# Norms and v issued later, blocks 12 to 15 choosing slots as four, and own buffers for the rows of blocks 16 to 21

## The chip, the cores and the metric

The kernel runs on one core of a Trainium2 chip. The core has five engines, each with its own queue of instructions that it works through in order: PE (TensorE, matrix products into PSUM), DVE (VectorE, elementwise work and reductions), ACT (ScalarE, copies out of PSUM and activations), POOL (GpSimd, masks, memory clearing, and the DMAs that scatter rows by an index) and SP (SyncE, which only issues the other DMAs). They wait for each other, and for DMAs, through semaphores. The metric is the device time of one execution in microseconds, lower being better.

## What is computed

A recurrence over 768 positions for 4 batches and 8 heads, whose result goes through a layer of 8 experts with one expert for each row:

```python
for t in range(S):                                   # _attn_ref: q, k, v of (4, 8, 768, 48)
    kt, vt, bt = (k_n[:, :, t], v[:, :, t], beta[:, :, t, None])     # k_n = k / (|k| + 1e-6)
    y[:, :, t] = np.einsum('bhd,bhde->bhe', q[:, :, t], state)
    v_old = np.einsum('bhde,bhd->bhe', state, kt)
    state = state + bt[:, :, :, None] * np.einsum('bhd,bhe->bhde', kt, vt - v_old)
...
x = attn_out.transpose(0, 2, 1, 3).reshape(B * S, H * D)             # 3072 rows of 384
logits = x @ w_gate                                                  # _moe_ref
expert_idx = np.argmax(logits, axis=1)
gate_w = probs[np.arange(N), expert_idx]                             # softmax of the logits
for e in range(E):
    h = np.maximum(x[expert_idx == e] @ w1[e], 0.0)                  # 384 x 1024
    out[expert_idx == e] = gate_w[mask, None] * (h @ w2[e])          # 1024 x 384
```

## The kernel before

The 768 positions are cut into 6 chunks (`tb`) of 128, and with 4 batches (`b`) this gives 24 blocks, `n = 4 * tb + b`, each for all 8 heads. The instructions of each engine are written out in the order in which the loop at line 1006 (`for t in range(NN + LAG)`) emits them; no scheduler moves them. A block lives for several steps `t`: in steps n to n+3 its four quarters of 32 positions go through `residual` and `apply`, quarter q in step n+q, so that each step holds quarters of four blocks. `residual(t)` makes PE compute what the state and earlier quarters predict (lines 451, 463), and DVE subtracts it from v (line 470). `apply(t)` multiplies by the inverse of a triangular matrix (line 478), and ACT copies the result out as u (line 483). `finish(n)` begins in step n+3: the output y (lines 498, 518), the update of the state (products 508, ACT copies st, line 512), the copy yt (522). Its last part runs in step n+4: PE turns y into a row of x together with the logits (line 548), ACT copies the row into a buffer (line 549), DVE reduces the logits (535).

Beside this run, a few pieces at each of the seven places of a step (`beside(t, i)`):

- `lanes(tb)`, the inverses of the next chunk, on DVE alone (lines 374 to 418), at counts fixed for each place; `prepare(tb)` before it, which also makes the norms of k. Line 351 turns the norms, line 354 writes them with four DMAs of 32 partitions into `nt_all`. In `scale_v` DVE scales v by them (line 428, every second step). v lies in a ring of 8 slots; `load_v(tb, q)` loads a quarter of a chunk into slots that `apply` of an earlier step was the last to read.
- `emit_slots`, the choice of slots. For a group of `w` blocks (4 up to block 11, pairs for 12 to 15, one from block 16 on) DVE finds each row's expert (lines 589 to 606), PE counts with a few products (line 559), DVE turns the counts into row numbers (625 `pos`, 650 `sli`), and POOL scatters each row to `xg` in DRAM by its number (line 658). The groups stand in a list `fine`, and after its first five steps only the group at the head of the list goes on. Groups of more than one block let out two scatters in a step.
- From step 20 on `pieces`: raw expert weights come in, ACT casts them to a high part (`w1h`, `w2h`, line 697) and DVE makes the low part (line 698). From step 23 on the first expert starts (`early`), for which line 737 reads `xg` back once all scatters up to block 17 have landed.

The buffers of the rows: two of two rows each for the first pair of a group (tag `row`), two for the second pair of a group of four (`rowb`). Blocks 16 to 21 use the two `row` buffers, one row at a time, in turns. A buffer is written again when the scatter that reads it has landed.

Steps are numbered by line 470: step 10 begins at 120.10 us of the trace, step 14 at 157.44, step 17 at 180.24, step 18 at 190.93, step 19 at 199.97, step 20 at 206.77, step 21 at 214.48, step 22 at 222.94, step 23 at 230.39, step 24 at 242.11. Behind step 26 come the eight experts, almost all on PE, up to 506 us.

Of the kernel before, what the change touches and what calls it, by code (L numbers as in the profile page):

```python
# [8 lines left out]
F32 = mybir.dt.float32  # L9
# [9 lines left out]
B, H, S, D = 4, 8, 768, 48  # L19
C = 128  # L20
NT = S // C
NB = C // 32
# [9 lines left out]
NN = NT * B  # L32
# [4 lines left out]
ROW = DM + E + 2  # L37
# [5 lines left out]
def deltanet_moe(ctx, tc, qT, kT, kr, v, beta, w_gate, w1, w2, out):  # L43
    nc = tc.nc
# [67 lines left out]
    W0 = 42  # L112
    WD = {1: 12, 2: 15, 3: 14, 4: 3}
    W1 = 8
    W4 = 12
    DM2 = 0
    DEF = 2
    AH = 3
# [12 lines left out]
    rp = ctx.enter_context(tc.tile_pool(name="rp", bufs=1, side="left"))  # L131
    lp_ = ctx.enter_context(ExitStack())
    ep_ = ctx.enter_context(ExitStack())
    lp = lp_.enter_context(tc.tile_pool(name="lp", bufs=1, side="left"))
    fp = ep_.enter_context(tc.tile_pool(name="fp", bufs=1, side="right"))
# [21 lines left out]
    nt_t = lp.tile([128, (NT * B + LAG) * H], F32, name="nt_all")  # L157
# [153 lines left out]
    def full(x):  # L311
        return x[:, 0:1024].rearrange("p (r c) -> p r c", c=32)
# [5 lines left out]
    def prepare(tb):  # L318

        T = tiles[tb]  # L320
        if tb == 0:
            T["lg"] = fp.tile([128, LW], F32, name="lg0", tag="lg", bufs=2)
            tiles["mark"] = nc.vector.transpose(out=full(T["lg"]), in_=tiles["dg"]).ins
            yield
        lg = T["lg"]
        lw = T["lw"]
        ss, s0, r0 = (lp.tile([128, 32], F32, name=f"{n_}{tb}", tag=n_) for n_ in ("ss", "s0", "r0"))
        nc.vector.tensor_scalar(out=ss, in0=lg[:, 0:1024:33], scalar1=1e-36, scalar2=None, op0=ALU.max)
        for _ in range(6 if tb > 1 else 1):
            yield  # L330
        nc.scalar.activation(out=s0, in_=ss, func=AF.Sqrt)
        yield
        nc.vector.reciprocal(r0, s0)
        yield
        nc.vector.tensor_tensor(out=r0, in0=r0, in1=ss, op=ALU.mult)
        yield
        nc.vector.tensor_tensor(out=s0, in0=s0, in1=r0, op=ALU.add)
        yield
        nc.vector.tensor_scalar(out=s0, in0=s0, scalar1=0.5, scalar2=1e-6, op0=ALU.mult, op1=ALU.add)
        yield  # L340
        nc.vector.reciprocal(r0, s0)
        yield
        nc.vector.tensor_tensor(out=ss, in0=r0, in1=bl[:, tb, :], op=ALU.mult)
        yield
        nc.vector.tensor_tensor(out=lw.rearrange("p a b -> p (a b)")[:, 0:1024:33], in0=ss, in1=r0, op=ALU.mult)
        yield
        nc.vector.tensor_tensor(out=r0, in0=ss, in1=r0, op=ALU.mult)
        yield
        def norms():
            sn = lp.tile([128, 32], F32, name=f"sn{tb}", tag="sn")  # L350
            nc.vector.transpose(out=sn, in_=s0)
            for q in range(NB):
                p = slice(32 * q, 32 * q + 32)
                nc.sync.dma_start(out=nt_t[p, (B * tb + q) * H:(B * tb + q) * H + 32], in_=sn[p])
            yield

        nc.vector.tensor_tensor(out=blocks(lg), in0=blocks(lg), in1=r0.rearrange("p (f r) -> p f r", f=2).unsqueeze(3)
                                .broadcast_to([128, 2, HB, HB]), op=ALU.mult)
        T["scaled"] = True
        yield  # L360
        yield from norms()
        T["nt"] = True

# [77 lines left out]
    def uview(n):  # L441
        return us[n].rearrange("t (h d) -> t h d", h=H)
# [44 lines left out]
    def finish(n):  # L487

        tb, b = n // B, n % B
        last = tb == NT - 1  # L490
        st, u = st_t[b], uview(n)
        qt, pm = qt_t[n % QTL], pm_t[n % QSL]
        yp = [pss.tile([128, 512], F32, name=f"yp{tb}_{b}_{j}", tag=f"y{j}")[:, 0:2 * C].rearrange("p (n c) -> p n c", n=2)
              for j in range(2)]
        for p in range(NP):
            for a in range(2):
                x = slice(64 * (a ^ p % 2), 64 * (a ^ p % 2) + 64)
                nc.tensor.matmul(yp[p % 2][x, p // 2], lhsT=st[64 * a:64 * a + D, p, 64 * a:64 * a + 64],  # L498
                                 rhs=qt[64 * a:64 * a + D, p, :], start=(p < 2), stop=True,
                                 tile_position=(64 * a, x.start), skip_group_check=True)  # L500
        if n + QTL < NN:
            load_qt(n + QTL)
        yield
        if not last:
            sb = sb_[b // 2][:, b % 2]
            for h in range(H):
                r = slice(64 * (h % 2), 64 * (h % 2) + D)
                nc.tensor.matmul(sb[r, h // 2, :], lhsT=tiles[tb][b]["kn"][:, h], rhs=u[:, h, :],
                                 start=(tb == 0 and b == 2 and h < 2), stop=True, skip_group_check=True)
            for a in range(2):  # L510
                r = slice(64 * a, 64 * a + D)
                nc.scalar.copy(out=st[r, :, r], in_=sb[r])  # L512
            if n + NB_ < NN - B:
                load_ku(n + NB_)
        yield
        for h in range(H):
            p, r = h // 2, 64 * (h % 2 ^ h // 2 % 2)
            nc.tensor.matmul(yp[p % 2][r:r + D, p // 2], lhsT=u[:, h, :], rhs=pm[:, h, :],  # L518
                             start=False, stop=True, skip_group_check=True)
        yt = lp.tile([128, NP, C], F32, name=f"yt{tb}_{b}", tag="yt", bufs=2)  # L520
        for j in range(2):
            nc.scalar.copy(out=yt[:, j::2], in_=yp[j])  # L522
        yield
        w = 1 if n >= NN - W1 else 2 if n >= W4 else 4
        j, m = n % w, min(w, 2)
        if j == 0:
            tiles["rows"] = []
            tiles["rl"] = lp.tile([128, w, E], F32, name=f"rl{tb}_{b}", tag=f"rl{w}", bufs=2)
        if j % m == 0:
            pool, tag = (fp, "rowb") if j >= 2 else (rp, "row") if n < NN - 2 else (xq_[0], "row")  # L530
            t = pool.tile([128, 2 if n < NN - 2 else 1, ROW], F32, name=f"row{tb}_{b}", tag=tag, bufs=2)
            tiles["rows"].append(t[:, 0:m])
        xp = emit_x(n, yt, tiles["rows"][-1][:, j % m])
        yield
        nc.vector.tensor_reduce(out=tiles["rl"][:, j], in_=xp[:, :, 2 * D:].rearrange("t p e -> t e p"), axis=AX.X, op=ALU.add)
        if j == w - 1:
            fine.append(emit_slots(tb, b - w + 1, w, tiles["rows"], tiles["rl"]))
# [192 lines left out]
    put, put_t, off = [], [], []  # L730
    wq, xq_, XR, last, psk_, fine, X0 = [], [], {}, [], [], [], {}
# [274 lines left out]
    for t in range(NN + LAG):  # L1006
        if t < NN and t % B == 0 and t > 0:
            while queue and queue[0][0] <= t // B:
                inverses(1, t)
            if t == NN - B:  # L1010
                ep_.close()
                wq.append(ep.enter_context(tc.tile_pool(name="wr", bufs=1, side="right")))
                xq_.append(ep.enter_context(tc.tile_pool(name="xq", bufs=1, side="right")))
                W = pieces()
                run(W)
        mask()
        residual(t)
        if LAG <= t < NN - KTL + LAG:
            load_kt(t - LAG + KTL)
        run(fin)  # L1020
        beside(t, 0)
        n = len(fine)
        run(fin)
        if len(fine) > n:
            tiles["at"] = 0
            run(fine[-1], 5)
        if B <= t + 1 < NN:
            scale_v(t + 1)
        if t < B - 1:
            clear_slots()  # L1030
        if t + 1 < NN + LAG and not B <= t + 1 < NN:
            scale_v(t + 1)
        if t + 1 < NN:
            clear_u(t + 1)
        beside(t, 1)
        dummy(WD.get(t, 0))
        copies = apply(t)
        run(copies, 2)
        for tb in range(1, NT):
            for i in range(NB):  # L1040
                if t == max(B * (tb - 1) + i - 1, 0):
                    load_v(tb, i)
        beside(t, 2)
        fin = finish(t - LAG) if t >= LAG else iter(())
        run(fin)
        chunk(qs_, t)
        beside(t, 3)
        run(fin)
        beside(t, 4)
        run(fin)  # L1050
        beside(t, 5)
        for _ in range(2 if t < 2 else 1):
            chunk(ks_, t)
        beside(t, 6)
        clear_slots()
    i = 0
# [141 lines left out]
    if True:  # L1198
# [20 lines left out]
        row = nc.values_load(gii[0:1, 0:1], min_val=0, max_val=E * N)  # L1219
# [51 lines left out]
        for f in range(KF):  # L1271
# [4 lines left out]
                                     in_=yo, in_offset=None, bounds_check=N - 1, oob_is_err=False)  # L1276
# [48 lines left out]
```

## Time and profile before

| | us |
|---|---|
| median of 3 runs (lowest to highest) | 518.15 (517.04 to 521.36) |
| the profiled execution | 522.53 |
| its span in the trace | 520.7 |
| PE busy in it | 484.5 (93%) |
| DVE busy | 337.7 (65%) |
| ACT busy | 254.7 (49%) |
| POOL busy | 112.8 (22%) |

All times of rows are microseconds from the start of the span. A row of the timeline gives the start, the time taken, the engine (PE is the matmul itself; its weight loads are a line of their own and not shown here), the line of the kernel, the operation, the tile written and those read, the shape, how many instructions are merged in the row, and in brackets how long the engine had been idle before it and what ended that. The start of a merged row is that of its first instruction. SPq is the queue of SP: for a DMA issue its time includes waiting that lies between merged issues. PEclk is the TensorE clock that was granted, as a share of the full 2.4 GHz; 0.50 is 1.2 GHz.

### The profile page before, as it was taken

The numbers are of one execution on the slowest core, as the hardware profiler recorded it, in microseconds if no ns is written. First come the engines' busy times: TensorE is split into PE (matmuls) and PEld (weight loads), VectorE is DVE, ScalarE is ACT, GpSimd is POOL, SyncE is SP. The second block draws the span as 40 slices with busy tenths as digits, with TensorE's granted clock in tenths as the row PEclk, the third lists the DMA queues.
The fourth block names the chain that finished last, engine by engine and source line by source line (L and its number), as shares of the span: only waits on it lengthen the run. The fifth ranks groups of instructions, "written<-read, shape, count | busy, mean of one in ns | idle before, by whom it ended". The sixth has DMA issues, their size and how long they took to land.

```text
span 520.7 us, 17340 instructions
## 1 busy us (share of the span) xinstructions
PE 484.5 (93%) x7286; PEld 434.8 (83%) x7291; DVE 337.7 (65%) x975; ACT 254.7 (49%) x539; POOL 112.8 (22%) x148
## 2 busy tenths in 40 slices
PE   7699899998998979999999999999999999999991
PEld 5656678887887868777889999999999999999991
DVE  2989959898689998465322976465756646565310
ACT  3413556674675645775343564444436444444210
POOL 6010121242242333323122001203030210303121
PEclk9999999997999989997999999999999999999997
DMA  6589747757554443762041595473847547481000
GB/s 197 121 194 256 188 140 192 220 157 183 145 156 107 136 121 107 244 198 91 18 102 68 163 239 157 121 183 115 203 124 164 160 134 161 141 197 36 13 18 27
DMA packets 74844, 74.14 MB, mean 142 GB/s; under 512 B 46649, under 2 KB 62506, under 8 KB 74764
## 3 DMA queue, kind: packets, MB, share of 16 engines
q1 hardware_dynamic: 71308, 63.45, 46.5%
q0 software_dynamic: 3456, 9.57, 5.1%
q8 instruction: 58, 0.95, 0.8%
q14 instruction: 22, 0.18, 0.1%
HBM read 54.25 MB, written 19.42 MB: 141 GB/s over the span
## 4 chain that ended last, share of the span: by engine, by line
PE 50%; issue 1%; ACT 1%; DMA 1%; SPq 1%; DVE 1%; POOL 1%; ACTq 0%; POOLq 0%
PE h L813 21%; PE y L824 18%; PE y L1131 4%; PE xp L548 1%; PE yp L518 1%; DMA w1r<-in_w_dram 1%; SPq L737 1%; PE ks L451 1%; PE ks L478 1%; PE pq L284 1%; PE ks L463 1%; PE xt L889 0%; POOL out_dram L827 0%; PE yp L498 0%; ACT pm L296 0%
## 5 line engine op out<-in xcount | busy, mean ns | idle before, releaser
L824 PE MATMUL y<-w2h,hx 128*128 128x384 f32 x352 | 93.2, 339 | 0.4 <-DVE hx L817 0.4
L827 POOL DMA_INDIRECT out_dram<-yo,idx x32 | 40.3, 1259 | 197.5 <-ACT yo L1126 113.0
L824 PEld LDWEIGHTS y<-w2h,hx 128*128 128x128 f32 x352 | 64.0, 188 | 1.2 <-DVE hx L817 1.1
L483 ACT COPY u<-ks 32x384 f32<-32x384 f32 x96 | 45.1, 469 | 33.7 <-PE ks L478 23.6
L813 PE MATMUL h<-xh,w1l 128*128 128x448 f32 x168 | 61.3, 365 | 0.0
L813 PE MATMUL h<-xh,w1h 128*128 128x448 f32 x168 | 61.2, 365 | 0.0
L813 PE MATMUL h<-xl,w1h 128*128 128x448 f32 x168 | 61.1, 363 | 0.0
L824 PE MATMUL y<-w2l,hx 128*128 128x384 f32 x176 | 59.4, 337 | 0.0
L698 DVE TENSOR_TENSOR w2l<-w2r,w2h 128x768 fp32r<-128x768 f32 x32 | 30.6, 957 | 40.6 <-ACT w2h L697 40.0
L817 DVE SCALAR_TENSOR_TENSOR hx<-h,hx 128x448 fp32r<-128x448 f32 (+1 forms) x64 | 37.5, 587 | 29.8 <-ACT hx L816 29.2
L816 ACT ACTIVATE hx<-h 128x448 fp32r<-128x448 f32 (+1 forms) x64 | 33.2, 518 | 44.8 <-PE h L813 44.8
L303 POOL TENSOR_SCALAR_AFFINE_SELECT pm<-pm 128x1024 f32<-128x1024 f32 x24 | 26.3, 1095 | 91.0 <-DVE tb L374 24.9
L1126 ACT ACTIVATE yo<-y,gt 128x384 f32<-128x384 f32 x22 | 12.8, 582 | 64.5 <-PE y L824 36.6
L451 PE MATMUL ks<-st,kt 112*32 112x96 f32 x768 | 43.5, 253 | 0.7 <-ACT st L512 0.5
L451 PEld LDWEIGHTS ks<-st,kt 112*32 112x32 f32 x768 | 32.4, 111 | 5.5 <-issue 1.9
L385 DVE TENSOR_TENSOR lw<-lw,ta 128x31 f32<-128x31 f32 (+7 forms) x96 | 36.6, 381 | 0.2
L284 PE MATMUL pg<-kt 48*128 48x128 f32 x384 | 31.7, 317 | 5.2 <-DMA kt<-in_kT_dram 4.2
L698 DVE TENSOR_TENSOR w1l<-w1r,w1h 128x1024 fp32r<-128x1024 f32 x24 | 29.4, 1225 | 9.0 <-ACT w1h L697 8.6
L478 PE MATMUL ks<-v_all,wt 32*32 32x48 f32 x1536 | 25.8, 206 | 10.1 <-DVE v_all L470 6.6
L284 PEld LDWEIGHTS pg<-kt 48*128 48x128 f32 x384 | 28.3, 222 | 8.3 <-issue 5.2
L658 POOL DMA_INDIRECT xg<-row,sli x22 | 22.6, 1028 | 58.0 <-ACT yt L522 20.4
L478 PEld LDWEIGHTS ks<-v_all,wt 32*32 32x32 f32 x1536 | 21.4, 107 | 16.4 <-DVE v_all L470 9.8
(166 smaller groups left out, 1038.3 us busy)
## 6 DMA issues: line engine op xcount, KB each, us to landing
w1r<-in_w_dram SPq DMA_DIRECT2D x24, 512.0 KB
w2r<-in_w_dram SPq DMA_DIRECT2D x32, 384.0 KB
xg<-zrow SPq DMA_DIRECT2D x14, 394.0 KB
kt<-in_kT_dram SPq DMA_DIRECT2D x24, 224.0 KB
qt<-in_qT_dram SPq DMA_DIRECT2D x24, 224.0 KB
xr<-xg SPq DMA_DIRECT2D x28, 168.0 KB
ku<-in_kr_dram SPq DMA_DIRECT2D x20, 192.0 KB
v_all<-in_v_dram SPq DMA_DIRECT2D x15, 192.0 KB
```

Of the source, the lines that this page charges most:

```text
L284: ins = nc.tensor.matmul(pg[a][:, p], lhsT=kt[r, p], rhs=xt[r, p], start=True, stop=True, tile_position=(64 * a, 0), skip_group_check=True)
L303: ins = nc.gpsimd.affine_select(out=pm, in_=pm, compare_op=ALU.is_gt, fill=0.0, base=0, pattern=[[0, H], [1, C]], channel_multiplier=-1)
L385: tiles["mark"] = noted(nc.vector.tensor_tensor(out=y, in0=y, in1=x, op=ALU.subtract))
L451: nc.tensor.matmul(ks[32 * q:32 * q + 32, 2 * p:2 * p + 2, :], lhsT=kt_t[n % KTL][0:RP, p, 32 * q:32 * q + 32], rhs=st_view(n % B, p), sta ...
L478: ins = nc.tensor.matmul(ks[r, h, :], lhsT=tiles[n // B]["wt"][r, n % B * H + h, :], rhs=vn[r, h, :], start=True, stop=True, tile_position ...
L483: nc.scalar.copy(out=uview(n)[r], in_=ks[r])
L698: nc.vector.tensor_tensor(out=lo, in0=src, in1=hi.bitcast(F32), op=ALU.subtract)
L813: nc.tensor.matmul(ps, lhsT=w[:, d, fs], rhs=x_[:, d], start=(n == 0), stop=(n == len(terms) - 1))
L816: nc.scalar.activation(out=hh, in_=ps, func=AF.Relu)
L817: nc.vector.scalar_tensor_tensor(out=hl, in0=ps, scalar=0.0, in1=hh.bitcast(F32), op0=ALU.max, op1=ALU.subtract)
L824: nc.tensor.matmul(ps, lhsT=h(f)[h_], rhs=w2[w][:, f, :], start=(n == 0), stop=(n == len(terms) - 1))
L827: nc.gpsimd.indirect_dma_start(out=out, out_offset=bass.IndirectOffsetOnAxis(ap=idx, axis=0), in_=yo, in_offset=None, bounds_check=N - 1, ...
```

## The change

Three edits:

1. The four DMAs of the norms, for chunks 2 to 5, are no longer issued where `prepare` ends, but put into the list `off`, due in step 4(tb-1)+1 at place 2; and a v quarter of chunks 2 to 5 is loaded one step later.
2. `W4` goes from 12 to 16, so blocks 12 to 15 choose slots as one group of four. No pairs are left.
3. Buffers: blocks 14 and 15 share one new buffer of two rows (`rowb`, in pool `lp`), and blocks 16 to 21 alternate between two new buffers of one row (`rowc`).

```diff
-    W4 = 12
+    W4 = 16
...
-            for q in range(NB):
-                p = slice(32 * q, 32 * q + 32)
-                nc.sync.dma_start(out=nt_t[p, (B * tb + q) * H:(B * tb + q) * H + 32], in_=sn[p])
+
+            def spread():
+                for q in range(NB):
+                    p = slice(32 * q, 32 * q + 32)
+                    nc.sync.dma_start(out=nt_t[p, (B * tb + q) * H:(B * tb + q) * H + 32], in_=sn[p])
+
+            if tb < 2:
+                spread()
+            else:
+                off.append(((B * (tb - 1) + 1, 2), spread))
+                off.sort(key=lambda x: x[0])
             yield
...
-            pool, tag = (fp, "rowb") if j >= 2 else (rp, "row") if n < NN - 2 else (xq_[0], "row")
-            t = pool.tile([128, 2 if n < NN - 2 else 1, ROW], F32, name=f"row{tb}_{b}", tag=tag, bufs=2)
+            pool, tag, k = ((fp if n < 12 else lp, "rowb", 2) if j >= 2 else (rp, "row", 2) if n < 16 else
+                            (lp, "rowc", 1) if n < NN - DEF else (xq_[0], "row", 1))
+            t = pool.tile([128, k, ROW], F32, name=f"row{tb}_{b}", tag=tag, bufs=1 if pool is lp and k > 1 else 2)
...
-                if t == max(B * (tb - 1) + i - 1, 0):
+                if t == (max(i - 1, 0) if tb == 1 else B * (tb - 1) + i):
                     load_v(tb, i)
```

What it moves, on DVE in step 17. `rl` is the reduction of block 13's logits, `v_all` with `nt_all` the scaling of v; the lines with `mx` to `ohb` are the pair's choice of experts. Before:

```order
L535 TENSOR_REDUCE rl_0_3551<-xp_1_3745 128x8
L589 TENSOR_REDUCE mx_0_3760<-rl_0_3551 128x2
L597 TENSOR_TENSOR row_0_3552<-rl_0_3551,mx_0_3760 128x2x8
L600 SCALAR_TENSOR_TENSOR oh_0_3763<-row_0_3552,rev_e 128x16
L603 TENSOR_REDUCE m_0_3765<-oh_0_3763 128x2
L606 TENSOR_TENSOR ohb_0_3767<-oh_0_3763,m_0_3765 128x16
L428 TENSOR_TENSOR v_all<-v_all,nt_all 128x768
```

The same place on DVE with the change (lines are numbered 9 higher here):

```order
L544 TENSOR_REDUCE rl_0_3550<-xp_1_3739 128x8
L436 TENSOR_TENSOR v_all<-v_all,nt_all 128x768
L382 TENSOR_TENSOR ta_6_3757<-lg_3467,lw_2661 128x175
L382 TENSOR_TENSOR tb_22_3759<-lg_3467,lw_2661 128x63
L393 TENSOR_TENSOR lw_2661<-lw_2661,ta_6_3757 128x25x7
```

The five instructions have left this step; they stand in step 19 now, where the choice of the pair 14, 15 stood, for four blocks at once.

On DVE, from the third cast `w1l` in step 21 to the first reduction in step 22. `row_0`, `row_1`, `row_2` with four-digit numbers from 4285 on are blocks 16, 17 and 18, and `pos`, `sli` ending in 0 and 1 are of blocks 16 and 17. Before:

```order
L698 TENSOR_TENSOR w1l_4396<-w1r_2_4399,w1h_4395 128x1024
L625 TENSOR_TENSOR pos_1_4561<-sb_97,ohb_1_4490 128x8
L632 SCALAR_TENSOR_TENSOR base<-lim,sb_97 128x8
L650 TENSOR_REDUCE sli_1_4579<-pos_1_4561 128x1
L470 TENSOR_TENSOR v_all<-v_all,ks_4596 128x384
```

With the change:

```order
L707 TENSOR_TENSOR w1l_4374<-w1r_2_4377,w1h_4373 128x1024
L634 TENSOR_TENSOR pos_0_4538<-sb_97,ohb_0_4302 128x8
L659 TENSOR_REDUCE sli_0_4555<-pos_0_4538 128x1
L634 TENSOR_TENSOR pos_1_4574<-sb_97,ohb_1_4461 128x8
L641 SCALAR_TENSOR_TENSOR base<-lim,sb_97 128x8
L659 TENSOR_REDUCE sli_1_4578<-pos_1_4574 128x1
L478 TENSOR_TENSOR v_all<-v_all,ks_4584 128x384
```

Slot 16 (`sli_0`), which stood a step earlier behind the first cast, now follows the third.

On POOL, steps 21 and 22 (u is cleared once in a step, `AFFINE_SELECT` is the mask of one block). Before:

```order
L658 DMA xg<-row_0_4303,sli_0_4415 24704x394
L303 AFFINE_SELECT pm_111<-pm_111 128x1024
L439 MEMSET u_4493 128x384
L658 DMA xg<-row_1_4475,sli_1_4579 24704x394
L303 AFFINE_SELECT pm_112<-pm_112 128x1024
```

With the change:

```order
L447 MEMSET u_4464 128x384
L667 DMA xg<-row_2_3940,sli_0_4292 24704x394 x2
L667 DMA xg<-row_0_4285,sli_0_4555 24704x394
L667 DMA xg<-row_1_4446,sli_1_4578 24704x394
L303 AFFINE_SELECT pm_112<-pm_112 128x1024
```

The scatters of blocks 14, 15 (`row_2_3940`), 16 and 17 now stand together behind the clearing of step 21; before, that of block 16 stood ahead of step 21's mask, and 14 and 15 in step 20.

## Rows read from the trace of the kernel before

**Rows 1.** Windows: stretch, length, busy us (instructions) per engine, PEclk, DMA share, GB/s.

```profile
core 0: us, PE busy (x) PEld busy (x) DVE busy (x) ACT busy (x) POOL busy (x), PEclk, DMA share, GB/s
...
120.10:132.00 11.90, 10.15 (x226) 8.60 (x226) 8.61 (x25) 5.76 (x13) 2.90 (x4) 0.71 0.56 133
157.40:166.00 8.60, 7.78 (x232) 6.80 (x232) 8.53 (x25) 5.57 (x14) 1.45 (x2) 1.00 0.54 116
180.20:190.90 10.70, 7.80 (x228) 6.61 (x226) 10.53 (x47) 5.16 (x13) 3.56 (x4) 1.00 0.53 151
190.90:200.00 9.10, 8.46 (x209) 7.45 (x210) 8.72 (x27) 4.11 (x10) 3.98 (x5) 0.63 0.36 108
...
230.40:242.10 11.70, 10.35 (x202) 8.44 (x202) 6.00 (x16) 6.62 (x15) 4.30 (x4) 0.71 0.52 164
...
300.00:500.00 200.00, 200.00 (x1063) 192.62 (x1062) 114.94 (x190) 91.17 (x151) 33.61 (x26) 1.00 0.53 139
```

**Rows 2.** Timeline of DVE in step 17, columns as told above.

```profile
182.71 0.17 DVE L589 TENSOR_REDUCE mx<-rl 128x2 f32<-128x16 f32 x1
...
183.63 0.95 DVE L428 TENSOR_TENSOR v_all<-v_all,nt_all 128x768 f32<-128x768 f32 x1
...
190.93 0.55 DVE L470 TENSOR_TENSOR v_all<-v_all,ks 128x384 f32<-128x384 f32 x1
```

**Rows 3.** Timeline, the waits of PE in step 18 and of DVE behind it.

```profile
191.54 1.50 PE L478 MATMUL ks<-v_all,wt 32*32 32x48 f32 x64 [2.77 <-DVE v_all L470]
...
199.97 0.56 DVE L470 TENSOR_TENSOR v_all<-v_all,ks 128x384 f32<-128x384 f32 x1 [0.31 <-PE ks L463]
```

**Rows 4.** Timeline of ACT, step 19.

```profile
205.29 0.20 ACT L630 COPY row<-ids 128x4 f32<-128x4 f32 x1
```

**Rows 5.** Timeline, steps 20 and 21: scatters of blocks 15 and 16, row 17.

```profile
210.67 0.97 POOL L658 DMA_INDIRECT xg<-row,sli  x1 [0.31 <-issue]
...
214.32 1.14 PE L548 MATMUL xp<-esel,yt 128*128 128x104 f32 x8
...
214.78 0.97 POOL L658 DMA_INDIRECT xg<-row,sli  x1 [3.13 <-DVE sli L650]
...
216.13 0.48 ACT L549 COPY row<-xp 128x384 f32<-128x384 f32 x1 [2.24 <-DMA xg<-row,sli]
```

**Rows 6.** Timeline, step 22, all engines, single rows.

```profile
222.78 1.14 PE L548 MATMUL xp<-esel,yt 128*128 128x104 f32 x8
222.79 0.16 DVE L650 TENSOR_REDUCE sli<-pos 128x1 int32<-128x8 f32 x1
...
223.72 0.99 POOL L658 DMA_INDIRECT xg<-row,sli  x1 [6.50 <-ACT yt L522]
...
224.00 0.48 ACT L549 COPY row<-xp 128x384 f32<-128x384 f32 x1 [1.16 <-issue]
...
225.28 1.16 PE L284 MATMUL pq<-qt,kt 48*128 48x128 f32 x16
...
226.62 0.17 PE L559 MATMUL sb<-ohb,ltri 128*128 128x8 bf16 x1
...
226.74 0.56 PE L508 MATMUL sb<-u,ku 128*48 128x48 f32 x16
...
228.77 0.63 ACT L512 COPY st<-sb 48x192 f32<-48x192 f32 x2
```

**Rows 7.** All scatters of line 658 from issue to landing, and SP's read of xg.

```profile
DMA to landing us min/median/max: 2.7/4.0/6.1
...
227.95 0.37 SPq L737 DMA_DIRECT2D xr<-xg  x1
```

**Rows 8.** Timeline: SP at a v load, and DVE's only wait before a scaling.

```profile
184.92 8.49 SPq L180 DMA_DIRECT2D v_all<-in_v_dram  x2
194.16 0.31 SPq L180 DMA_DIRECT2D qt<-in_qT_dram  x1
...
218.12 0.96 DVE L428 TENSOR_TENSOR v_all<-v_all,nt_all 128x768 f32<-128x768 f32 x1 [0.29 <-issue]
```

**Rows 9.** Windows of 1 us for PE around the third fall of the clock.

```profile
235.00:236.00 1.00, 0.39 (x2) 0.61 0.73 271
...
242.00:243.00 1.00, 1.00 (x12) 0.97 0.00 0
```

## What is expected of the change, and why

> **What bounds the kernel now.** I read the busy times stage by stage first. From 300 to 500 us PE is busy for all 200 of 200 us at a granted clock of 1.00 [rows 1]: the expert part is pure PE work, nothing of the change reaches it, and whatever the first part gains or loses moves the end by the same amount. So the question is when the recurrence ends. I number its steps by the subtraction of line 470; step 17 begins at 180.24, step 22 at 222.94. In its middle the bound alternates. Step 14 (157.4 to 166) has DVE busy for 8.53 of 8.6 us, step 17 (180.2 to 190.9) for 10.53 of 10.7 [rows 1]: DVE works through the inverse of the next block and is late with its subtraction; PE then stands idle 2.77 us before the products of line 478 [rows 3]. Behind step 19 the inverses are over and the chain goes through ACT: the row copy, the casts of expert weights, the copies u, st, and what PE does with them.
>
> Next the granted clock. It falls to 0.50, that is to 1.2 GHz, three times: the mean is 0.71 in step 10 (120.1 to 132.0), 0.63 in step 18, 0.71 in step 23 [rows 1]. The third fall lies between 235 and 242.1 [rows 9]; 0.71 over 11.7 us means 11.7 x 0.29 / 0.5 = 6.8 us at half speed. Against step 14, of the same kind of work without a fall, step 10 costs 3.3 us and step 18 0.5 (DVE is the bound there anyway); in step 23 PE is busy all the while, so up to 3.4 us are lost. Together about 7.2.
>
> Own time: the profiled execution took 522.53 us (span 520.7). The median of the three runs shown is 518.15, 4.4 less. As estimate from the falls: a median run had about one of the two dear falls, not all. I state the sum against both.
>
> **Norms and v later: nothing, either way.** In before, SP sits 8.49 us in a v load that waits for the last reader of its ring slots; the next load, a qt, issues at 194.16 [rows 8], but it waits for PE's line 498 by itself. So nothing useful stood behind the blocked load. On the other side, of all scalings of v by the norms (the only readers of both) DVE's single idle time is 0.29 us, put down to issue [rows 8]; none waits for a DMA. The new order takes away one step of lead, some 9 us by the steps of [rows 1], and leaves at least one whole step between a load of v or norms and its scaling. Cost 0; the cover is that step. Were it gone, a late load would stand in front of a scaling and the subtraction behind it. Four norm copies move behind one v load on SP and ahead of a qt that waits anyway.
>
> **Step 17: a gain of 1.0.** The pair 12, 13 no longer chooses there. Five DVE instructions go, from 182.71 to the scaling at 183.63: 0.92 us [rows 2], and one pos of the kind of the 0.16 us sli [rows 6]; pipelined, some 0.1. DVE is the bound of this step, so line 470 of step 18 comes 1.0 earlier, and PE's idle time shrinks from 2.77 to about 1.8. Step 18 is DVE's too: its last line 470 had idled only 0.31 for PE [rows 3]. So -1.0 stands at step 19. The bounds: 0.9 (only the five) and 1.3 (PE's 0.31 also gone, if the clock does not fall at 190).
>
> **Steps 19 and 20: about nothing.** In step 19 four blocks choose instead of two: the same number of DVE instructions, four more small PE products of the 0.17 us kind [rows 6] that overlap each other, three more small ACT copies of 0.20 [rows 4] ahead of yt. Over steps 17 to 21 PE has one product fewer and ACT two copies more. Bounds -0.2 and +0.7 (all four in sequence); I take 0, since row 205.29 is followed by a copy whose product is queued behind PE's own work.
>
> **Step 21: a gain of 0.6.** Row 17 stood in the buffer of the pair 14, 15 and ACT waited 2.24 us for that scatter; it wrote at 216.13 [rows 5]. Its product xp began at 214.32; a row copy that waits for PE alone starts 1.22 after (222.78 to 224.00 [rows 6]), so 215.54. In the new buffers this wait is gone: ACT's chain (cast, u, pm, cast) and with it DVE's last cast w1l of this step come 0.6 earlier.
>
> **Step 22: a new wait, and the term that decides.** Rows 16 and 18 share one of the two new buffers (16 to 21 alternate), as they shared one before. Before, block 16 was scattered at 214.78, so at 224.00 its buffer was long free. Now the queue of slot choices stands behind the group of four, whose second pair is let out only in step 21: blocks 14, 15, 16 and 17 leave POOL one after the other, and slot 16 is computed behind the third cast w1l, in the place where slot 17 was (222.79, scatter at 223.72 [rows 6]). So scatter 16 starts at 223.72 - 1.0 - 0.6 = 222.1. ACT's copy of row 18 waits for its landing. How long that is, the scatters show: 2.7 at least, 4.0 median, 6.1 at most from issue to landing [rows 7]; and in this very place the read of xg, which waits for every scatter up to block 17, issued at 227.95 [rows 7], so that landing took at most 4.2. I take 4.0: row 18 at 226.1, against 224.00 before and 222.4 if it did not wait. The wait is 3.7 us.
>
> What is queued behind it: ACT's cast, the u copies and st (228.77), DVE's reduction and slot choice of 18, and PE's count product at 226.62, behind which line 508 (226.74) stands in order [rows 6]. All of step 22 hangs on this copy, so everything moves to 226.1 - 224.00 = +2.1 against before: both gains are eaten. With 2.7 us it is +0.8, with 6.1 +4.2.
>
> A rule of the Trainium skill speaks for the short end. Its page "DMA: Bandwidth & Descriptors", section "Anatomy of one DMA — SWDGE (gpsimd) path", gives a DMA issued from GpSimd about 2.0 us plus its bytes at 436 GB/s; for 128 rows of 394 words that is an estimate of 2.5 us, and the sum would be +0.6 instead of +2.1. The trace has no scatter that fast (2.7 is its least).
>
> **The clock in step 22.** PE's last work ahead of the wait, pq, ends at 225.28 + 1.16 = 226.44 in before [rows 6], 224.8 to 225.1 after; line 508 moves to 228.8. PE is idle for some 3.7 us, longer than the 2.77 us at 191, after which the clock stood at 0.50. So I expect a fall here, of the same 6.8 us, about 229 to 236. Its first 2.5 us lie beside ACT's chain to the end of st (228.77 + 0.63 + 2.1 = 231.5); the other 4.3 us are PE work at half speed and lose 2.2. Some 0.3 come on top, as lines 508 and 518 at half speed no longer end ahead of st: 2.5. With PE behind at half speed, the fall of step 23 is then likelier to be absent (-3.4 where before has it).
>
> **The sum.** Own time: 522.53 + 2.1 + 2.5 - 3.4 = 523.7. Median: if its one fall was that of step 23, 518.15 + 2.1 + 2.5 - 3.4 = 519.4; if it was that of step 10, 518.15 + 2.1 + 2.5 = 522.8. I take the middle, 521.0, and this case's own range 519.4 to 522.8.
>
> **Rivals.** (a) *Early landing*: scatter 16 lands in 2.7 us, the wait is 2.4, PE's idle time like that of step 17, and a fall takes the place of another: 518.15 + 0.8 = 519, between 517.5 and 519.4. For it: minimum of rows 7; against: weight loads run beside it, and the median. By its estimate of 2.5 us the page of the Trainium skill named above would give this case too. (b) *The wait is off the path*: if ACT's copy does not hold step 22, only gains are left, 518.15 - 1.6 = 516.5, and 513 if the fall of step 23 goes as well. For it: a scatter may leave earlier than I think; against: slot 16 comes after the third cast on DVE, and ACT works in order. (c) *Slower*: the scatter lands late, since four follow each other on POOL beside the w2 loads. With 6.1 us: 518.15 + 4.2 + 2.5 = 524.9. It decides from 4.5 us on, where the dear half of the forecast (522.8) passes 523.3. For it: the pair 14, 15 in step 20, beside w1 loads, held ACT until 216.13, 5.5 us after the issue at 210.67 [rows 5]. (d) *The norms and v do matter*: a stall of DVE at a scaling; nothing in rows 8 speaks for it, and it goes into (c).
>
> **Chances.** Forecast 0.56; (a) 0.15; (b) 0.11; (c) with (d) 0.18. A measurement of this kernel can tell about 1% from no change, 513.0 to 523.3. Under 513.0 falls half of (b), 0.06; over 523.3 falls (c) and nothing else, 0.18; the rest, 0.76, is the same. For 8 in 10 the range goes from 516.0 (into (b)) to 525.0 (the end of (c)).
>
> **What would show it.** Right: step 17 about 9.7 us with DVE full; no wait of ACT's row copy in step 21; in step 22 a wait of 3 to 4 us of that copy for the scatter of block 16, PE idle beside it and a granted clock of 0.50 behind. Wrong: row 18 written less than 1.5 us after its product, or a scaling of v that waits for a DMA, or a scatter of 16 ahead of the third cast.

## The result, and the profile after

The changed kernel took 524.75 us (median; 520.42 to 530.52), the kernel before beside it 519.44 us (516.02 to 521.88). The ratio is 1.0084, with a 95% interval of 1.006 to 1.0108: slower by 0.8%, inside the 1% that the prediction called the same, and inside its range. Five of the twenty runs of the changed kernel lie over 1.5% above its fastest and are left out of the ratio as slow, so by the ratio the change costs some 4.4 us, while the two medians are 5.3 apart. The forecast was +2.9 us against the median then known.

The profiled executions can't simply be set against each other: that of after took 520.42 us, its quickest of all, that of before 522.53, above all twenty runs of its kernel. Over steps 17 to 23 the two are only 1.4 us apart (63.31 and 61.87), with one fall of the clock in after and two in before, so this pair doesn't hold the whole loss. The steps are read one by one. This is the view by windows of after, of its steps 17, 18, 20, 21 and 22 (length, busy us and instructions of each engine, granted clock, DMA share, GB/s), as [rows 1] shows it of before:

```profile
core 0: us, PE busy (x) PEld busy (x) DVE busy (x) ACT busy (x) POOL busy (x), PEclk, DMA share, GB/s
...
176.53:185.40 8.87, 8.22 (x224) 6.80 (x224) 8.87 (x40) 4.83 (x12) 2.48 (x4) 1.00 0.45 133
185.40:193.96 8.56, 6.66 (x216) 5.80 (x216) 8.49 (x24) 4.72 (x12) 1.45 (x2) 1.00 0.27 78
...
201.99:210.18 8.19, 7.71 (x220) 6.34 (x220) 4.01 (x9) 5.64 (x12) 3.79 (x5) 1.00 0.85 256
210.18:221.68 11.50, 7.88 (x222) 6.42 (x221) 5.39 (x17) 6.65 (x15) 5.19 (x5) 1.00 0.73 213
221.68:229.70 8.02, 7.28 (x221) 6.33 (x222) 3.63 (x11) 6.14 (x14) 0.56 (x2) 1.00 0.43 139
```

Step 17 is 8.87 us with DVE full, against 10.7 [rows 1]. Not all of these 1.8 us are the change's. The first instruction of DVE behind the subtraction takes 1.02 us in before, beside POOL's mask, and 0.29 in after, where PE let DVE wait for 1.16 us and the mask was over by then. That is 0.7 us, and 1.1 remain for the choice that left the step. Before, and after:

```profile
180.49 1.09 POOL L303 TENSOR_SCALAR_AFFINE_SELECT pm<-pm 128x1024 f32<-128x1024 f32 x1 [1.39 <-DVE tb L374]
180.71 1.02 DVE L385 TENSOR_TENSOR lw<-lw,ta 128x135 f32<-128x135 f32 x1
```

```profile
175.53 1.09 POOL L303 TENSOR_SCALAR_AFFINE_SELECT pm<-pm 128x1024 f32<-128x1024 f32 x1 [0.67 <-DVE tb L382]
176.53 0.55 DVE L478 TENSOR_TENSOR v_all<-v_all,ks 128x384 f32<-128x384 f32 x1 [1.16 <-PE ks L471]
177.00 0.29 DVE L393 TENSOR_TENSOR lw<-lw,ta 128x135 f32<-128x135 f32 x1
```

Step 21 is 11.50 us, with PE busy for 7.88 of them; in before the step, from 214.48 to 222.94, is 8.47 long. There, far more than in step 22 (8.02 against 7.44), the loss stands. The timeline of DVE and of PE in that step (start, us, engine, line, operation, and in brackets the idle time ahead and what ended it):

```profile
216.24 1.23 DVE L707 TENSOR_TENSOR w1l<-w1r,w1h 128x1024 fp32r<-128x1024 f32 x1 [1.61 <-ACT w1h L706]
217.38 0.16 DVE L634 TENSOR_TENSOR pos<-sb,ohb 128x8 f32<-128x8 f32 x1
```

```profile
217.59 0.17 PE L568 MATMUL sb<-ohb,utri 128*128 128x8 bf16 x1 [2.30 <-DVE pos L634]
...
219.80 0.21 PE L471 MATMUL ks<-u,gg 128*32 128x48 f32 x1 [0.44 <-issue]
220.52 0.30 PE L471 MATMUL ks<-u,gg 128*32 128x48 f32 x5 [0.35 <-issue]
221.25 0.26 PE L459 MATMUL ks<-st,kt 112*32 112x96 f32 x1 [0.43 <-issue]
221.52 1.14 PE L557 MATMUL xp<-esel,yt 128*128 128x104 f32 x8
```

In before, pos of block 16 ran in step 20, and the count of block 17 in step 21 followed PE's other work with no wait:

```profile
213.65 0.16 DVE L625 TENSOR_TENSOR pos<-sb,ohb 128x8 f32<-128x8 f32 x1
...
217.89 0.18 PE L559 MATMUL sb<-ohb,utri 128*128 128x8 bf16 x1
```

The reader is to see two things. First a wait: PE wants to count block 17 into `sb`, the running counts in PSUM. But pos of block 16 must have read these counts before, and pos 16 stands on DVE behind the third weight cast (216.24, itself waiting for ACT). PE is idle for 2.30 us, and all products behind the count with it. Second, the 80 small products of `ks` that follow don't run through: three times PE pauses 0.35 to 0.44 us, with nothing shown that it waits for. The subtraction of step 22 waits 3.47 us for them:

```profile
221.68 0.55 DVE L478 TENSOR_TENSOR v_all<-v_all,ks 128x384 f32<-128x384 f32 x1 [3.47 <-PE ks L471]
```

The wait that the prediction named is there too, but small. ACT and POOL, same view:

```profile
210.92 0.48 ACT L558 COPY row<-xp 128x384 f32<-128x384 f32 x1 [1.56 <-PE xp L557]
...
223.32 0.48 ACT L558 COPY row<-xp 128x384 f32<-128x384 f32 x1 [5.60 <-DMA xg<-row,sli]
```

```profile
218.51 0.97 POOL L667 DMA_INDIRECT xg<-row,sli  x1 [2.89 <-DVE sli L659]
```

Row 17 (210.92) no longer waits for a scatter, as it did in [rows 5]. Row 18 does, and the number in its bracket is large. But ACT would have idled anyway: its product xp began at 221.52 only, and a row copy that waits for PE alone comes 1.22 later [rows 6], at 222.74. The landing of scatter 16 costs 0.6 us of the 5.60. In `after_2`, a second profile of the same kernel, row 18 waits for its product alone.

Why is pos 16 so late? The slot choices of all blocks stand in one waiting line, and only its first entry runs. A group of four scatters its second pair one step after the first (the `while tiles["t"] == t1` in `emit_slots`) and stays at the head of the line till then. In before, the pair 14, 15 left it in step 20, and block 16's pos came in that step too. Now the group of 12 to 15 holds it until step 21.

### The profile page after: what moved, and what is told of

It reads as the page before. It is cut to its first block, busy times and chain, and to the rows that moved or that the text cites. A ratio compares the mean times of both kernels' runs of the same rounds, so it can differ in the third digit from the quotient of the medians.

```text
span 518.7 us, 17333 instructions
## 1 busy us (share of the span) xinstructions
PE 481.0 (93%) x7290; PEld 429.7 (83%) x7290; DVE 338.3 (65%) x968; ACT 254.8 (49%) x541; POOL 113.1 (22%) x148
## 4 chain that ended last, share of the span: by engine, by line
PE 48%; DVE 2%; ACT 1%; issue 1%; SPq 1%; DMA 1%; POOL 1%; ACTq 0%; POOLq 0%; DVEq 0%
PE h L822 21%; PE y L833 18%; PE y L1140 4%; PE xp L557 1%; SPq L746 1%; DMA w1r<-in_w_dram 1%; PE yp L526 1%; DVE v_all L441 0%; PE ks L486 0%; PE ks L459 0%; PE ks L471 0%; PE pq L284 0%; PE xt L898 0%; POOL out_dram L836 0%; DVE w2l L707 0%
## 5 line engine op out<-in xcount | busy, mean ns | idle before, releaser
L459 PE MATMUL ks<-st,kt 112*32 112x96 f32 x768 | 45.0, 249 | 2.5 <-issue 1.5
L284 PE MATMUL pg<-kt 48*128 48x128 f32 x384 | 32.9, 317 | 5.0 <-DMA kt<-in_kT_dram 3.5
L707 DVE TENSOR_TENSOR w1l<-w1r,w1h 128x1024 fp32r<-128x1024 f32 x24 | 30.6, 1275 | 9.6 <-ACT w1h L706 9.1
L822 PEld LDWEIGHTS h<-xh,w1l 128*128 128x128 f32 x168 | 31.6, 188 | 2.6
L822 PEld LDWEIGHTS h<-xl,w1h 128*128 128x128 f32 x168 | 31.6, 188 | 2.5
```

What stands on the lines that cost most here:

```text
L284: ins = nc.tensor.matmul(pg[a][:, p], lhsT=kt[r, p], rhs=xt[r, p], start=True, stop=True, tile_position=(64 * a, 0), skip_group_check=True)
L459: nc.tensor.matmul(ks[32 * q:32 * q + 32, 2 * p:2 * p + 2, :], lhsT=kt_t[n % KTL][0:RP, p, 32 * q:32 * q + 32], rhs=st_view(n % B, p), sta ...
L707: nc.vector.tensor_tensor(out=lo, in0=src, in1=hi.bitcast(F32), op=ALU.subtract)
L822: nc.tensor.matmul(ps, lhsT=w[:, d, fs], rhs=x_[:, d], start=(n == 0), stop=(n == len(terms) - 1))
```

## The experiments

All ratios are to the kernel before, run beside on the same chip, with 95% intervals. Five theories stand against each other. The row theory is the prediction's: row 18 waits for the landing of scatter 16. The count theory: PE's count 17 waits for pos 16. The line theory is the same with its cause, the waiting line. The load theory: norms and v come too late. The clock theory: nothing in particular, the schedule only shifts against falls of the granted clock and gaps.

**The two halves apart.** `vn_only` has the edits of norms and v alone, `slots_only` the rest:

```
vn_only:    W4 = 12, rows as before;  spread() put off and load_v later, as in the change
slots_only: W4 = 16, rows as in the change;  norms and load_v as before
```

> The kernel before with the first edit alone: norms and v issued later. Row theory (the loss is ACT's copy of row 18 waiting for the scatter of block 16) and count theory (the loss is PE's count product of block 17 waiting for DVE's pos of block 16 behind the third weight cast): both say no change, ratio 0.997 to 1.003, no wait of a scaling of v for a DMA. Load theory (the later loads cost): ratio 1.005 to 1.010.

> The group of four and the new row buffers alone, norms and v as before. Row theory and count theory: the whole loss is here, ratio 1.005 to 1.011, step 21 some 11 us long with PE idle over 2 us before its count product of block 17. Load theory: ratio 0.996 to 1.000.

Measured: `vn_only` 518.92 us, 0.9994 (0.997 to 1.0019); `slots_only` 526.72 us, 1.0115 (1.0079 to 1.0152). The whole loss is in the slots and rows; the load theory falls.

**A third buffer for the rows.** `three_buffers` takes away what row 18 waits for:

```diff
-bufs=1 if pool is lp and k > 1 else 2)
+bufs=1 if pool is lp and k > 1 else 3 if tag == "rowc" else 2)
```

> The changed kernel with three instead of two buffers for the rows of blocks 16 to 21, so that row 18 has one that no scatter reads. Row theory as it stands in the prediction: 3.7 us of wait go, ratio to before 0.996 to 0.999. Count theory: only the last 0.6 us of ACT's wait goes, the 2.3 us of PE before its count product stay, ratio 1.004 to 1.009.

Measured: 522.74 us, 1.010 (1.0062 to 1.0139). PE's wait, DVE's behind it, and row 18:

```profile
217.48 0.17 PE L568 MATMUL sb<-ohb,utri 128*128 128x8 bf16 x1 [2.67 <-DVE pos L634]
```

```profile
221.83 0.55 DVE L478 TENSOR_TENSOR v_all<-v_all,ks 128x384 f32<-128x384 f32 x1 [3.74 <-PE ks L471]
```

```profile
223.75 0.48 ACT L558 COPY row<-xp 128x384 f32<-128x384 f32 x1 [6.15 <-PE xp L557]
```

Row 18 now waits for its product and no longer for a DMA, and nothing is won. As the explanation of the loss, the row theory falls.

**The third cast later.** `cast_late` lets pos 16 pass ahead of it; `before_cast_late` is the same move in the kernel before:

```diff
-    WSL = (..., (21, 1), (21, 3), (22, 1), ...)
+    WSL = (..., (21, 1), (21, 6), (22, 1), ...)
```

> The changed kernel with the third weight cast moved from place 3 of step 21 to place 6, behind the slots of blocks 16 and 17. Count theory: pos of block 16 no longer stands behind the cast on DVE, PE's 2.3 us go, scatter 16 leaves over 2 us earlier and row 18's wait goes with it, ratio 0.995 to 1.001, step 21 about 8 us. Row theory: scatter 16 leaves earlier too, a similar ratio. Load theory: ratio 1.005 or more.

> The kernel before with its third weight cast moved from slot 3 to slot 6 of step 21, the move that took 2 us from the changed kernel's step 21. Line theory: here no count of PE waits for a pos behind that cast, so the move is worth nothing: step 21 at 8.0 to 8.7 us, time 0.998 to 1.002 of before. Cast theory (the cast stands badly in slot 3 in any kernel): 0.994 to 0.997 of before.

Measured: `cast_late` 524.26 us, 1.0048 (1.0013 to 1.0083). In its profile PE's count 17 has no wait, and step 21 is 9.69 us. That is less than the count theory expected (0.995 to 1.001, step 21 about 8 us). By the point estimates about half of the loss is gone, but the interval overlaps that of the changed kernel (1.006 to 1.0108), so a gain isn't shown. The 80 products of `ks` (a window of these alone) still take 4.13 us, with PE busy for 2.73:

```profile
216.75:220.88 4.13, 2.73 (x80) 1.89 (x80) 0.00 (x0) 0.00 (x0) 1.00 0.81 235
```

Its step 22 is 11.94 us long, with the clock at 0.50 for most of it.

`before_cast_late`: 521.95 us, 1.0033 (0.9999 to 1.0068), with step 21 at 11.11 us. I had expected nothing, and was wrong: where PE isn't late, the moved cast stands in front of the subtraction of step 22, and PE waits for that:

```profile
223.25 1.82 DVE L698 TENSOR_TENSOR w1l<-w1r,w1h 128x1024 fp32r<-128x1024 f32 x1 [2.39 <-ACT w1h L697]
225.00 0.54 DVE L470 TENSOR_TENSOR v_all<-v_all,ks 128x384 f32<-128x384 f32 x1
```

```profile
225.59 0.60 PE L478 MATMUL ks<-v_all,wt 32*32 32x48 f32 x36 [2.24 <-DVE v_all L470]
```

**The buffers alone, and the lateness alone.** `rowc_only` is the kernel before with the two new buffers. `pair_late` adds one thing: the scatters of 14 and 15 are held to step 21, so that block 16's slots come behind the third cast though there is no group of four.

```diff
             if w > 1 and j % 2 == 0:
+                while n1 == 16 and (tiles["t"], tiles["at"]) < (21, 3):
+                    yield
                 while tiles["t"] == t1 ...
```

> The kernel before with two buffers of their own for rows 16 to 21 alone; slots of blocks 12 to 15 in pairs as before. Line theory: step 21 at 7.8 to 8.6 us, row 18 waits under 1 us since scatter 16 stays in step 20; time 0.998 to 1.001 of before. Row theory (the buffers themselves cost time, by row 18's wait for scatter 16): step 22 at 9 us or more and 1.003 to 1.008 of before.

> The kernel before with two buffers of their own for rows 16 to 21, as rowc_only, and one thing more: the scatters of rows 14 and 15 are held back to step 21, so that block 16's slots come behind the third weight cast as in the changed kernel. No group of four on blocks 12 to 15, norms and v as before. Line theory: step 21 at 11 to 12 us with PE waiting 2 to 3 us for pos of block 16; time 1.004 to 1.010 of before, 3 to 4 us above rowc_only. Clock theory: no more than 1 us above rowc_only.

> pair_late again, whose first comparison (1.0024, 0.9988 to 1.0061) could not tell between the theories. Line theory: step 21 and 22 together 2 to 4 us above rowc_only's 15.3, time 1.002 to 1.007 of before. If the lateness of block 16 costs only together with the group of four: 0.998 to 1.002, though step 21 is long.

Measured: `rowc_only` 521.18 us, 1.0007 (0.9966 to 1.0049): the buffers are neutral, to within 0.5%. Its step 21 is 7.83 us, 0.6 under before, and its step 22 is 7.44, not the 9 or more of the row theory. `pair_late` 520.54 us, 1.0024 (0.9988 to 1.0061): below what the line theory expected (1.004 to 1.010), with an interval too wide to decide; on another chip (`pair_late_2`) 522.53 us, 1.0074 (1.0041 to 1.0107). In both profiles the wait is made again without the group of four:

```profile
223.01 0.17 PE L560 MATMUL sb<-ohb,utri 128*128 128x8 bf16 x1 [2.67 <-DVE pos L626]
```

```profile
218.16 0.17 PE L560 MATMUL sb<-ohb,utri 128*128 128x8 bf16 x1 [2.68 <-DVE pos L626]
```

So the lateness is enough to make the wait, and step 21 is then 10.29 and 12.03 us. It is enough for a measurable loss in one of two comparisons.

**The line opened.** `four_early` keeps the group of four, but its second pair is scattered in the same step as the first, so that block 16 follows in step 20:

```diff
-            if w > 1 and j % 2 == 0:
+            if w > 1 and (j == 0 or j == 2 and n1 < 16):
                 while tiles["t"] == t1 ...
```

> The changed kernel, but the second pair of rows of blocks 12 to 15 is scattered in the same step as the first, instead of one step later. The slot choices wait in one line, first come first served, so block 16's stand in step 20 again, ahead of block 17's count. Line theory (the loss is made by block 16's slots being held back behind the group of four until after the third weight cast): step 21 at 8.0 to 8.7 us instead of 11.5, PE's count of block 17 without a wait, row 18 waiting less than 1 us for the landing of scatter 16; time 0.996 to 1.001 of before, as step 17's 1.1 us stays gained. Clock theory (the loss is made by falls of the granted clock and gaps in PE that any shift of the schedule brings): step 21 is short, but the time stays at 1.006 to 1.012 of before.

> four_early again, beside the changed kernel on the same chip. Line theory: 0.996 to 1.002 of before and 0.6 to 1.1% below after_2; step 21 at 7.8 to 8.7 us. Clock theory: within 0.3% of after_2.

> The changed kernel again, for comparison on the same chip. Line theory: 1.006 to 1.011 of before, step 21 at 11 to 12 us, with PE waiting 2 to 3 us for pos of block 16 and gaps without a shown reason in the products behind it. Clock theory: the time is the same, but step 21's length does not repeat.

Measured, first: 519.69 us, 1.000 (0.9967 to 1.0034), as the line theory expects. In the second comparison, on another chip beside the changed kernel: 523.41 us, 1.0101 (1.0071 to 1.0132), and the changed kernel (`after_2`) 524.54 us, 1.0104 (1.0062 to 1.0146). The two comparisons of one kernel exclude each other. The second came out as the clock theory expected, within 0.3% of `after_2`; and `after_2` came out as the line theory expected, its step 21 11.75 us long with a wait of 2.68 for pos 16. Both profiles of `four_early` have no wait for pos 16. They differ in step 20, where five scatters (12 to 16) now follow each other. Windows of the 80 `ks` products of that step, first execution and second:

```profile
211.27:213.34 2.07, 2.05 (x80) 1.70 (x80) 0.00 (x0) 0.00 (x0) 1.00 0.95 354
```

```profile
205.37:212.94 7.57, 4.68 (x80) 2.78 (x80) 0.00 (x0) 0.00 (x0) 0.82 0.92 288
```

The second execution's products come in small bunches, with eight pauses of 0.21 to 0.42 us; three of them, and the subtraction that waits behind:

```profile
206.87 0.40 PE L459 MATMUL ks<-st,kt 112*32 112x96 f32 x4 [0.38 <-issue]
207.61 0.40 PE L459 MATMUL ks<-st,kt 112*32 112x96 f32 x4 [0.34 <-issue]
...
210.60 0.41 PE L471 MATMUL ks<-u,gg 128*32 128x48 f32 x5 [0.42 <-issue]
```

```profile
213.03 0.56 DVE L478 TENSOR_TENSOR v_all<-v_all,ks 128x384 f32<-128x384 f32 x1 [5.10 <-PE ks L471]
```

Step 20 takes 12.60 us there instead of 8.09. The loss has left step 21 and come back in step 20. So opening the line is no sure cure, the line theory is not the whole, and the part of the clock theory that speaks of gaps in PE is not refuted.

**Idle products against the fall of the clock.** `four_early` showed the granted clock at 0.50 from 197.2 to 204.0, behind PE's two waits for DVE in steps 18 and 19. `four_early_fill` puts eight products without use into each wait:

```diff
-    WD = {1: 12, 2: 15, 3: 14, 4: 3}
+    WD = {1: 12, 2: 15, 3: 14, 4: 3, 18: 8, 19: 8}
```

> four_early with eight idle products of 128x512 more on PE at each of the two places where it waits for the subtraction of v (1.9 us each, steps 18 and 19 of the trace); their results are not used. If the fall of the granted clock that follows these waits (197.2 to 204.0 us in four_early) goes away with them and PE is what step 19 waits for: step 19 at 6.8 us instead of 9.6, time 0.992 to 0.997 of before. If the fall only moves to another step: 0.998 to 1.002. If the idle products end behind the subtraction, each step is longer by what they overhang, and the time is 1.001 to 1.004.

Measured: 522.88 us, 1.008 (1.0049 to 1.0111), outside all three expectations and no better than `four_early_2` beside it. Its windows from the last microsecond of step 17 to the end of step 20:

```profile
186.00:196.00 10.00, 9.89 (x235) 7.62 (x236) 9.93 (x30) 4.98 (x12) 1.61 (x3) 1.00 0.29 88
195.60:202.76 7.16, 7.16 (x224) 5.67 (x223) 6.64 (x18) 4.54 (x15) 1.64 (x3) 1.00 0.23 63
202.76:215.32 12.56, 9.64 (x220) 7.18 (x220) 3.22 (x12) 5.83 (x13) 8.31 (x9) 0.90 0.83 274
```

The clock holds 1.00 in steps 18 and 19. But `four_early_2` had no fall there either, so the products prove nothing about it. Step 20 has the same bunches again, 12.56 us long. No version beat the kernel before by more than its interval.

**All profiles side by side**: length of five steps in us, from subtraction to subtraction in each trace, and the ratio. Blocks 12 to 15 choose as pairs in the upper six.

| kernel | 17 | 18 | 20 | 21 | 22 | ratio |
|---|---|---|---|---|---|---|
| before | 10.69 | 9.03 | 7.70 | 8.47 | 7.44 | 1 |
| vn_only | 9.98 | 8.65 | 8.56 | 8.11 | 7.75 | 0.9994 |
| rowc_only | 10.69 | 9.41 | 8.53 | 7.83 | 7.44 | 1.0007 |
| before_cast_late | 10.47 | 10.41 | 7.70 | 11.11 | 9.91 | 1.0033 |
| pair_late | 10.22 | 9.37 | 7.22 | 10.29 | 8.34 | 1.0024 |
| pair_late_2 | 10.10 | 9.14 | 7.22 | 12.03 | 7.44 | 1.0074 |
| after | 8.87 | 8.56 | 8.19 | 11.50 | 8.03 | 1.0084 |
| after_2 | 8.87 | 8.57 | 8.55 | 11.75 | 8.62 | 1.0104 |
| slots_only | 8.86 | 8.57 | 8.52 | 11.93 | 12.17 | 1.0115 |
| three_buffers | 8.86 | 8.57 | 7.97 | 11.85 | 8.60 | 1.010 |
| cast_late | 8.87 | 8.57 | 7.98 | 9.69 | 11.94 | 1.0048 |
| four_early | 8.86 | 8.57 | 8.09 | 7.83 | 7.44 | 1.000 |
| four_early_2 | 8.87 | 8.57 | 12.60 | 8.99 | 7.74 | 1.0101 |
| four_early_fill | 8.86 | 8.57 | 12.56 | 9.10 | 7.73 | 1.008 |

**What is shown, and what stays open.** Shown: the loss belongs to the group of four with the rows, the buffers alone cost nothing, and row 18's wait isn't it. In every profile where block 16's slots come behind the third cast (the cast unmoved), PE waits 2.30 to 2.68 us. Argued, from one or two profiles of each kernel: the rest comes from PE's pauses in the `ks` products and from the clock behind the wait. The nearest like with like are before and `after_2` (profiled at 525.03 us, close to its median), each with two falls of the clock in steps 17 to 23: there step 17 gives -1.8, 18 -0.5, 20 +0.9, 21 +3.3, 22 +1.2 and 23 +0.3, together +3.2. Ahead of them step 16, which the table leaves out, gives +1.3. It is 8.37 to 10.28 us in the eight and 7.16 to 8.80 in the six, mostly by the same pauses: nine profiles have them there, among them `vn_only` and `pair_late_2`. Open: why these pauses come in one execution of a kernel and not in another, and with that how the 4.4 us divide. The test that would tell, scatters 14 and 15 in step 21 but block 16's slots let past them, was not run.

## Why the prediction was right or wrong, point by point

**Norms and v: right.** `vn_only` is at 0.9994, and no scaling of v (line 436) waited for a DMA in after.

**Step 17: right.** Forecast -1.0. Step 17 is 8.86 to 8.87 us in all eight profiles with the group of four, and 9.98 to 10.69 in the six without. The six differ by the instruction beside POOL's mask; with 0.29 us for it in each they are 9.96 to 10.06, and the gain is 1.1 to 1.2. Step 18 is 8.56 to 8.57 against 8.65 to 10.41. PE's wait for DVE, 2.77 in [rows 3], was to shrink to about 1.8: it is 1.89 in `four_early`, and 0.88 in after, where a pause made PE itself late.

**Steps 19 and 20: right within their bounds.** Step 19 is 6.80 us in `after_2` and 6.81 in before (8.03 in after, where the clock fell). Step 20 of before and of `rowc_only` lie at 7.70 and 8.53, so the 8.19 of after shows no cost; `after_2`, with two pauses in its `ks` products, has 8.55.

**Step 21: the step that failed.** The prediction gave it -0.6, for row 17's wait. That wait went, and where only the buffers changed (`rowc_only`) the step is indeed 7.83 instead of 8.47. But the same text says that "slot 16 is computed behind the third cast w1l", and it priced only the scatter that follows. It did not ask who else waits for pos 16: PE's count 17, which overwrites the counts that pos reads. That is the missing term, put at nothing without a reason: +2.3 to +2.7 of wait, and with the pauses behind it step 21 came out at +3.0 instead of -0.6.

**Step 22, the term that was to decide: right mechanism, wrong size.** Row 18 waits for scatter 16 in after, as forecast, but 0.6 us instead of 3.7, and not at all in `after_2`. It came 1.80 us after its product began, so the prediction's sign of being wrong (under 1.5) did not show, and the wait of 3 to 4 us that was to show it right did so only in the bracket of ACT's row. The landing was nearly right: forecast 4.0, and issue 218.51 to row 223.32 is 4.8 at most. The Trainium skill, "DMA: Bandwidth & Descriptors", section "Anatomy of one DMA — SWDGE (gpsimd) path", would make it an estimate of 2.5 us; the measurement decides against that here. What made the wait small is the other end: PE itself was late, so the product wasn't there either. Rival (a), a landing in 2.7 us, falls with that, since the wait ended with the landing; rival (b), "the wait is off the path", came true for a reason that it didn't have, and without its gain.

**The clock: the fall came, a step earlier.** It was expected behind PE's new idle time. That idle time stands in step 21, 2.30 us long in the profile of after, with no fall behind; in the five profiles where it was 2.67 or 2.68 us, the clock fell to 0.50 within 1.1 us of its end. The length alone doesn't decide: a fall follows PE's wait of 2.24 us in `before_cast_late`, and none a wait of 2.32 in step 18 of `vn_only`. `after_2`, windows ahead, in and behind:

```profile
219.00:220.50 1.50, 1.01 (x40) 0.98 (x42) 0.96 (x6) 0.62 (x3) 0.09 (x1) 1.00 0.86 295
220.50:227.40 6.90, 6.00 (x136) 4.82 (x131) 1.54 (x8) 1.45 (x3) 3.33 (x4) 0.51 0.35 117
227.40:229.00 1.60, 1.60 (x34) 1.31 (x27) 0.91 (x2) 1.54 (x4) 0.00 (x0) 1.00 0.08 15
```

What it costs varies: step 22 is 8.62 us there and 12.17 in `slots_only`, where the clock stood at 0.50 for twice as long, against 8.03 in after without a fall. The -3.4 for step 23 was too much: step 23 is 9.70 us in `pair_late` without a fall and 11.72 in before with one, so 2.0. That the fall of step 23 would then be absent came true in some profiles (after, `slots_only`, `pair_late`) and not in others (`after_2`, `three_buffers`).

**The sum** was nearer than its terms, and that is partly luck: +2.9 forecast, +4.4 measured, because a wait of 3.7 us was put into the wrong step, where 2.3 to 2.7 us and pauses stood in another, beside a fall of the clock that came in five of the six profiles with that wait. The range held for the uncertainty of a landing that in the end did not matter.

## What to carry to other kernels

When a step is delayed, list everyone who waits for each of its instructions, also those who want to overwrite what it reads: a running count in PSUM makes the next block's write wait for this block's read. A waiting line that only runs its head carries one group's delay to all that stand behind it. And a fix should be timed more than once and on more than one chip: here one kernel gave 1.000 on one and 1.0101 on another, though whether the chip makes the difference isn't shown.

## What the runs showed of the hardware

I had not expected PE's pauses in the `ks` products. Undisturbed, the 80 products of a step take 1.72 us. The table gives, from the packets of the scatters' DMA queue in the traces, the share of the 16 DMA engines that this queue held during the products; these are the products of step 21 if not said otherwise:

| kernel | products, us | scatters' share |
|---|---|---|
| before | 2.54 | 0.00 |
| pair_late | 2.36 | 0.18 |
| four_early, step 20 | 2.07 | 0.24 |
| after | 3.85 | 0.29 |
| pair_late_2 | 4.09 | 0.32 |
| after_2 | 4.05 | 0.33 |
| cast_late | 4.13 | 0.34 |
| slots_only | 4.24 | 0.35 |
| three_buffers | 4.12 | 0.35 |
| four_early_2, step 20 | 7.57 | 0.34 |
| four_early_fill, step 20 | 7.53 | 0.35 |

In before 0.49 us of the 2.54 are a wait for ACT's st, and `pair_late` and `four_early` have no pause. The passes of this table with a share of 0.29 or more are slow, some in part by a granted clock of 0.50, and all with pauses, some 0.74 us apart. It is no law: in step 18 of `vn_only` the scatters held 0.17 and the products took 2.98 with two pauses, and in step 17 of `four_early` they held 0.52 and the 80 products took 1.72, without a pause:

```profile
183.09:184.81 1.72, 1.72 (x80) 1.51 (x80) 0.00 (x0) 0.00 (x0) 1.00 0.88 275
```

The pauses carry the mark "issue", so what PE lacks in them no profile here shows. Nearest to it, the Trainium skill ("Runtime: NRT & Kernel Launch", section "Instruction fetch mechanics") says that an engine fetches its instructions by a DMA queue of its own and that this is mostly hidden. If the pauses are such fetches, the profile should show them, since it lists two DMA queues of the kind "instruction" (packets, MB, share of the 16 engines' time). Over all of `four_early_2`:

```profile
q8 instruction: 58, 0.95, 0.8%
q14 instruction: 22, 0.18, 0.1%
```

As an estimate, q8 is PE's: PE's 14,575 products and weight loads are 251 for each of its 58 packets, and the other engines have far fewer instructions. From 206.80 to 212.65 us, where seven of the eight pauses of that execution lie, the same view lists only loads (q1) and scatters (q0):

```profile
q1 hardware_dynamic: 472, 0.75, 46.9%
q0 software_dynamic: 318, 1.01, 44.4%
```

So no packet of that kind moves beside these seven pauses, which speaks against fetches as their cause. What the cause is stays open.
